# Neighborhood attention on one core: V's lower shift in one DMA, and a band's loads issued earlier

## The chip, the cores and the metric

The kernel runs on one core of a Trainium2 chip. The metric is device time in microseconds (us), from one launch to its end. Engines are named as the profile names them: PE is TensorE's matmul (PEld its weight load), DVE is VectorE, ACT is ScalarE, POOL is GpSimd, and SP is SyncE, which here only issues DMAs.

## The reference

The image is 224 x 224 with 192 channels in bf16. Every pixel attends to 49 neighbours, a 7 x 7 window with dilation 2, shifted inward at the edges. There is one head.

```
qkv = x @ wqkv;  q, k, v = split(qkv)
r0 = clip(row - 6, 0, H - 13);  c0 = clip(col - 6, 0, W - 13)
neighbours of (row, col): rows r0 + 2a, columns c0 + 2b,  a, b in 0..6
p = softmax(q . k[neighbours] * C**-0.5)
out = (p @ v[neighbours]) @ wo
```

## The kernel before

Because of the dilation a pixel sees only pixels of its own row parity (apart from the edges), and the same for columns. The work is therefore cut into a row class `rc` (2), a column class (2) and tiles of 8 x 8 queries of one class. The weights are folded at the start: the logits are x times G, where G is computed from x and wq wk', and the values carry wv wo in them, so that no separate output projection is left.

**Steps and pairs.** There are 14 *steps* (`n` in the code), one for a band of 32 image rows and a row class: `steps[n] = (ti, rc)`. A step has 7 *pairs* (`m` = 0 to 6), and the main loop runs over all 98 pairs with a running number `k`. A pair has two slots (`ab`), each a column of two 8 x 8 query tiles for both column classes. For a pair the kernel does:

- `stage1`: matmuls of x and G into the logits (line 499), and the row maximum on DVE (line 501).
- `stage1b`: the exponential on ACT (line 508), once for each slot.
- `stage2`: the transpose of the probabilities, on PE with a copy by DVE (lines 538 and 539), or, for pairs 4 and 5 of steps 2 to 10 (table `TURN`), by a DMA transpose on SP's queue (line 522).
- `stage3`: the product with V (line 549), three pairs later (`LAG = 3`).
- `stage4`: division by the row sum on DVE (lines 555 and 572) and an output DMA, on SP's queue for most (line 578), from six rotating buffers `o_sb`.

**Background work.** Between the stages of the current pairs the kernel prepares the next step: G's tiles (`g_items`; evacuated by ACT, part of it copied on by POOL, line 450) and V's 14 blocks (`v_item`; matmuls in lines 335 and 338, evacuated by ACT or DVE, lines 326 and 328). Which item runs behind which pair is written out by hand in the strings `BACK` (steps 2 to 11) and `LATE`. The preparation of a step begins in pair 3 of the step before it and ends in pair 2 of the step itself. In `BACK` the items v0 to v6 come up to the first item of pair 6, v7 and v8 later in pair 6, v9 in pair 0, and v10 to v13 in pair 1.

**V's lower shift.** A step's keys are two half-bands of eight rows. V is kept in two tiles for each row class, and each newly made V has its lower 64 partitions copied into the lower partitions of the other tile (`v_over`, line 349). The 14 blocks stand at places 0 to 13 of a tile, and the list `AT` says which block stands where: a slot s reads the places `AT[s - 1]` and `AT[s]`, so that the first slot of a step reads the places 7 (block 13) and 0, and the eighth is the first that reads place 8. The list `vs` makes the blocks in the order 0 to 6, 13, 7 to 12, so that its first eight items, v0 to v7, fill the places 0 to 7. `back` starts the shift in parts, when the last item of a part has been evacuated.

**Loads.** A band of x is read from HBM by three DMA transposes on SP's queue (`load_items`, line 154): tile `x1`, from which POOL copies the `xb` rows (line 160) and sorts columns into `xs` (line 170), and the two `xa` tiles. `x1` has two buffers, so the load of band n + 3 overwrites that of band n + 1, which POOL must have read. The list `ld` holds the three loads of a step, and one is taken off and issued at the end of each of the pairs 0, 1 and 2.

**What sets the order.** Each engine runs its instructions in the order of the program (`in_order`). SP's queue holds, in that order, the outputs, V's shift, the loads and the DMA transposes of the probabilities; each issue also waits until the DMA issued eight places before it has landed. POOL's queue holds the copies of G, V's last shift, the copies and sorts of x, and the output DMAs of the first slot of a step (line 601).

Of the kernel before, what the change touches and what calls it, by code (L numbers as in the profile page):

```python
# [99 lines left out]
def kernel(  # L100
# [44 lines left out]
    def load_items(b):  # L145

        src = xp[16 * b:16 * b + 16].rearrange("r j c -> (r j) c")
        at = (16 * b) % (2 * RP) * S

        def one(k):  # L150
            if k == 1:
                X1[b] = x1_p.tile([128, BND], BF, name=f"x1_{b}", tag="x1")
            dst = X1[b][:] if k == 1 else XA[k // 2][:, at:at + BND]
            nc.sync.dma_start_transpose(out=dst.unsqueeze(1), in_=src[:, 128 * k:128 * k + 128])  # L154

        return [lambda k=k: one(k) for k in ((0, 2, 1) if b in (0, 2, 3) else (1, 0, 2))]
# [183 lines left out]
    def v_item(rc, ti, cb):  # L340
        def emit(dve):
            pv = ps_g.tile([128, 512], F32, name="pv", tag="pg")
            v_mms(pv, lambda k, h: XS[rc][:, k, cb, 64 * h:64 * h + 64])
            evac(_win(VV[rc][ti % 2], 0, 128, AT[cb] * VP, [[193, 2], [1, C]]), pv[:, 0:2 * C].rearrange("p (t c) -> p t c", c=C), dve)
        return emit

    def v_over(rc, ti, c0, c1, eng=nc.sync.dma_start):

        eng(out=VV[rc][1 - ti % 2][0:64, c0:c1, :], in_=VV[rc][ti % 2][0:64, c0:c1, :])
# [126 lines left out]
    def stage1(J, ab):  # L476
        s = 2 * J.m + ab
        s_ps = SS[ab]


        cols = {0: [(1, 7, S - 7), (8, 8, 0)], 2: [(1, 15, 9)]}.get(s, [(2, 14, 8 * s - 6)])
        lo = cols[0][0]
        for cc in range(2):
            units = []
            for h in range(2):
                u = []
                for pas in range(2):
                    X = (XA, XB)[pas][cc]
                    for (v, k0, n) in key_rows(J, h):
                        for (q, nq, c) in cols:  # L490
                            o = _win(s_ps, 64 * h, 64, cc * 256 + 16 * k0 + q, [[16, n], [1, nq]])
                            u.append((n * nq, o, G[J.rc][cc][:, pas, s, 64 * h:64 * h + 64], _win(X, 0, 128, _x(J.rc, v, c), [[RW, n], [1, nq]]), pas))
                units.append(u)
            done = [0, 0]
            while units[0] or units[1]:
                h = 0 if units[0] and (done[0] <= done[1] or not units[1]) else 1
                (cols_, o, w, r, pas) = units[h].pop(0)
                done[h] += cols_
                nc.tensor.matmul(o, lhsT=w, rhs=r, start=(cc == 0 and done[h] == cols_), stop=(cc == 1 and not units[h]), skip_group_check=True)  # L499
        nmx = stat.tile([128, 2], F32, name="nmx", tag="nmx")  # L500
        nc.vector.tensor_reduce(out=nmx[:], in_=_win(s_ps, 0, 128, lo, [[256, 2], [16, 16], [1, 16 - lo]]), axis=AX.XY, op=ALU.max, negate=True)  # L501
        J.p = PP[J.k % 3]
        J.s[ab] = (s_ps, nmx)

    def stage1b(J, ab):
        s_ps, nmx = J.s[ab]
        for cc in range(2):
            nc.scalar.activation(out=J.p[:, ab, cc].rearrange("p q (r k) -> p q r k", k=8), in_=_win(s_ps, 0, 128, cc * 256, [[8, 2], [16, 16], [1, 8]]),  # L508
                                 func=ACTF.Exp, bias=nmx[:, cc:cc + 1], scale=1.0)
# [3 lines left out]
    def turned(J):  # L513
        return J.m in TURN[J.n]
# [97 lines left out]
    def g_all(n):  # L612
        ti, rc = steps[n]
        its = [g_items(rc, ti, s0, ns) for (s0, ns) in GROUPS]
        return [it for (w0, w1, h) in its for it in (w0, w1)], [h for (w0, w1, h) in its]
# [31 lines left out]
    def pool_do(n):  # L647
        for _ in range(min(n, len(pool_q))):
            pool_q.pop(0)()
# [51 lines left out]
    ld, gw, vs = [], [], []  # L701

    def back(it, by_dve):
        it(by_dve)
        for (i, c0, c1) in ((7, 0, 8), (10, 8, 11), (13, 11, 14)) if nb == 0 or nb >= 11 else ((6, 0, 6), (9, 6, 10), (13, 10, 14)):
            if it in vs and it is vs[i]:
                v_over(rcb, tib, c0, c1, pool if nb >= 11 or nb > 0 and i in (13,) else nc.sync.dma_start)

# [6 lines left out]
    for k in range(NP + 2):  # L715
        J = pairs[k] if k < NP else None
        n = J.n if J else NSTEP
        w64, w128 = [], []
        if J:
            m = J.m  # L720
            nb, mb = divmod(k - LAG, 7)
            bg = k >= LAG and nb + 1 < NSTEP
            if bg and mb == 0:
                tib, rcb = steps[nb + 1]
                gw, gh = g_all(nb + 1)
                vs = [v_item(rcb, tib, cb) for cb in (0, 1, 2, 3, 4, 5, 6, 13, 7, 8, 9, 10, 11, 12)]
            if n == 0:
                w64 = gh0[m + 1:m + 2] if m < 3 else gh[mb // 2:mb // 2 + 1] if mb % 2 == 0 else []
                w64 = [(it, False) for it in w64]
            elif bg:  # L730
                w = [(({"g": gw, "h": gh, "v": vs}[t[0]][int(t[1:].rstrip("de"))], t[-1] == "d" or t[-1] == "e" and turned(pairs[k - 1])) if t != "-" else None) for t in (SECOND if nb == 0 else BACK if nb < 11 else LATE)[mb].split()]
                w64, w128 = [it for it in w[:1] if it], w[1:]
            stage1(J, 0)
            stage1(J, 1)
            stage1b(J, 0)
            if m == 0 and n + 3 < NBAND:
                ld = load_items(n + 3)
        if k == NP:
            stage2(pairs[k - 1])
        late = [pairs[i] for i in values_of(k)]  # L740
        for A in late[:1]:
            stage3(A, 0)
            stage3(A, 1)
            if k >= NP:
                stage4a(A, 0)
                stage4a(A, 1)
            stage4(A, 0)
            if k == NP - 1:
                stage4a(A, 1)
        for (it, by_dve) in w64:  # L750
            back(it, by_dve)
        if J:
            stage1b(J, 1)
        if J and turned(J):
            stage2(J)
        if 1 <= k < NP and not turned(pairs[k - 1]):
            stage2(pairs[k - 1])

        if late and n > 0:
            stage4(late[0], 1)  # L760
        for A in late[1:]:
            stage3(A, 0)
            stage3(A, 1)
            stage4(A, 0)
            stage4(A, 1)
        if not J:
            continue

        for w in PLAN[m].split() if n == 0 else ():
            (kind, by), at = w.split(":")[0], [int(c) for c in w.split(":")[1:]]  # L770
            if kind in "VWGH":
                {"V": v0, "W": vs, "G": gw0, "H": gw}[kind][at[0]](by == "d")
            elif kind == "N" and late:
                stage4(late[0], 1)
            elif kind == "X":
                xb_items(2, act if by == "a" else dve)[at[0]]()
            elif kind == "R":
                v_over(0, 0, at[0], at[1], nc.scalar.dma_start if by == "a" else nc.sync.dma_start)
            elif kind == "T":
                v_over(rcb, tib, at[0], at[1], nc.scalar.dma_start if by == "a" else nc.sync.dma_start)  # L780
        for (it, by_dve) in w128:
            back(it, by_dve)
        if ld:
            ld.pop(0)()
        if n == 0 and m == 1:
            first_vd()
            g_row_on(1, 2, 12)
            g_col_on()
        for q in range(2):
            if (n, m) == ((1, 3), (1, 5))[q]:  # L790
                marks_on(q)
        add = [it for c in FIRST[k] for it in first_pool(c)] if k < len(FIRST) else []
        if n > 1:
            if m == 3 and n + 2 < NBAND:
                add = sort_items(n + 2, J.rc, pool)
            if m in (2, 4) and n + 3 < NBAND:
                srt = sort_items(n + 3, J.rc, pool)
                add = srt[:2] if m == 4 else xb_items(n + 3, pool) + srt[2:]
        pool_q[:0] = add
        if n == 12 and m == 1:  # L800
            last = ((0, 9, 0, 1), (9, 7, 9, 0))
            g_col(1, 6, 0, 1, pool)
            g_row(1, 6, 0, 1, pool, last)
            g_row(1, 6, 1, 13, pool, last[1:])
        pool_do(max(4 if n < NSTEP - 1 else 8, len(add)))
# [34 lines left out]
```

## Time and profile before

| | |
|---|---|
| median of 3 runs | 339.31 us |
| the three runs | 339.48, 337.97, 339.31 us |
| the profiled execution | 337.53 us |
| its span, first to last instruction | 335.8 us |
| granted TensorE clock, mean over the span | 0.996 |
| moved by DMA | 55.78 MB, mean 166 GB/s |
| SP's DMA queue, share of 16 engines' span | 84.6% |

The durations below come from the one profiled execution, which was faster than two of the three timed runs. Its span is shorter than its time by what lies before the first instruction and after the last one. In lines of a timeline the columns are start and duration in us, engine and line of the kernel, operation, output and input tile, and in brackets the idle time before it with what ended it. In lines of a list of groups they are line, engine, operation, tiles, shapes and count, then busy us and the mean ns of one, then the idle time before. In a list of waits they are total us, number of times, and the longest.

### The profile page before, as it was taken

How to read it: one execution, taken by the hardware profiler on the slowest of the kernel's cores; microseconds unless marked ns; L12 is line 12 of the kernel's file. 1: busy time of each engine (PE TensorE's matmuls, PEld its weight loads, DVE VectorE, ACT ScalarE, POOL GpSimd, SP SyncE). 2: the span in 40 equal slices, each digit the busy share in tenths (PEclk: the TensorE clock that was granted, in tenths of full speed). 3: DMA queues.
4: the chain of work that ended last, by engine and by line, in shares of the span. 5: the costliest groups of instructions: out<-in, count | busy, mean ns of one | idle time of the engine just before them, and what ended most of it. 6: DMA issues, size and time to landing. Idle time of an engine off the chain costs nothing.

```text
span 335.8 us, 18841 instructions
## 1 busy us (share of the span) xinstructions
PE 318.4 (95%) x7820; PEld 292.8 (87%) x7820; DVE 310.0 (92%) x729; ACT 307.4 (92%) x809; POOL 287.1 (86%) x428
## 2 busy tenths in 40 slices
PE   4699999999999999999999999999999999999982
PEld 3578898999999999998999999989999889999871
DVE  8859999989999999999999999999999999999993
ACT  7679899999999999898999999999999999999992
POOL 8499999899987989789699797997987977997765
PEclk9999999999999999999999999999999999999998
DMA  9999745999999899799997997989989978758934
GB/s 186 215 165 193 141 112 128 208 198 194 182 186 187 160 190 176 140 221 149 169 187 175 179 184 176 163 155 198 174 154 184 182 144 130 143 115 154 149 88 111
DMA packets 143368, 55.78 MB, mean 166 GB/s; under 512 B 117113, under 2 KB 141138, under 8 KB 143283
## 3 DMA queue, kind: packets, MB, share of 16 engines
q1 hardware_dynamic: 138203, 51.98, 84.6%
q0 software_dynamic: 4416, 1.81, 3.0%
q8 instruction: 61, 1.00, 1.2%
q10 hardware_dynamic: 664, 0.80, 1.1%
q14 instruction: 24, 0.20, 0.2%
HBM read 0.29 MB, written 19.27 MB: 58 GB/s over the span
## 4 chain that ended last, share of the span: by engine, by line
PE 80%; ACT 6%; DVE 4%; DMA 3%; SPq 3%; issue 1%; POOL 1%; POOLq 0%; DVEq 0%; ACTq 0%
PE s L499 18%; PE o_ps L549 17%; PE pg L415 13%; PE pv L335 10%; PE pv L338 9%; PE pt_ps L538 7%; PE pgh L415 7%; ACT p L508 3%; SPq L154 3%; DVE nmx L501 2%; DMA pt_sb<-p 2%; DMA xa<-in_x_dram 2%; ACT v L328 1%; ACT g L328 1%; ACT gx L328 1%
## 5 line engine op out<-in xcount | busy, mean ns | idle before, releaser
L508 ACT ACTIVATE p<-s,nmx 128x256 bf16<-128x256 f32 x392 | 163.5, 486 | 15.4 <-DVE nmx L501 13.7
L501 DVE TENSOR_REDUCE nmx<-s 128x2 f32<-128x448 f32 (+1 forms) x196 | 114.3, 624 | 8.9 <-PE s L499 4.5
L572 DVE TENSOR_TENSOR o_sb<-o_ps,rs 128x384 bf16<-128x384 f32 x169 | 94.2, 558 | 5.9
L499 PEld LDWEIGHTS <-g 128*64 128x64 bf16 x2592 | 86.8, 110 | 7.0 <-issue 1.9
L328 ACT CAST v<-pv 128x384 bf16<-128x384 f32 x180 | 85.5, 513 | 2.9 <-PE pv L338 2.4
L499 PE MATMUL s<-xa,g 128*64 128x196 bf16 (+8 forms) x1296 | 83.0, 217 | 1.0 <-ACT p L508 1.0
L499 PE MATMUL s<-xb,g 128*64 128x196 bf16 (+8 forms) x1296 | 82.8, 217 | 0.2 <-ACT g L328 0.2
L549 PE MATMUL o_ps<-v,pt_sb 128*64 128x193 bf16 x1456 | 81.2, 246 | 0.2 <-DMA pt_sb<-p 0.2
L335 PE MATMUL pv<-wb,xs 128*64 128x384 bf16 x406 | 74.6, 333 | 3.7 <-ACT xs L360 3.1
L338 PE MATMUL pv<-wp,xs 128*64 128x192 bf16 x812 | 75.3, 250 | 0.1
L450 POOL COPY g<-gx 64x512 bf16<-64x512 bf16 (+1 forms) x110 | 61.9, 563 | 14.7 <-ACT gx L328 10.6
L601 POOL DMA_DIRECT2D out_dram<-o_s x120 | 68.4, 576 | 3.5 <-issue 2.6
L549 PEld LDWEIGHTS <-pt_sb 128*64 128x64 bf16 x1456 | 66.5, 109 | 0.3 <-DMA pt_sb<-p 0.3
L415 PEld LDWEIGHTS <-aw 128*64 128x64 bf16 x1320 | 58.9, 111 | 8.3 <-issue 2.3
L338 PEld LDWEIGHTS <-xs 128*64 128x64 bf16 x812 | 60.4, 112 | 6.3
L328 ACT CAST g<-pg 128x512 bf16<-128x512 f32 (+4 forms) x130 | 53.8, 480 | 1.4 <-PE pg L415 0.8
L415 PE MATMUL pg<-xb,aw 128*64 128x512 bf16 (+9 forms) x440 | 55.0, 272 | 0.0
L415 PE MATMUL pg<-xa,aw 128*64 128x512 bf16 (+9 forms) x440 | 53.4, 273 | 1.5 <-ACT gx L328 0.9
L170 POOL COPY xs<-xa 128x896 bf16<-128x896 bf16 x51 | 46.6, 941 | 5.5 <-DMA xa<-in_x_dram 4.7
L538 PE MATMUL pt_ps<-ident,p 128*64 128x128 bf16 x1072 | 45.5, 219 | 0.0
L539 DVE COPY pt_sb<-pt_ps 128x1024 bf16<-128x1024 bf16 x63 | 42.9, 681 | 0.3 <-DMA out_dram<-o_sb 0.2
L335 PEld LDWEIGHTS <-xs 128*64 128x64 bf16 x406 | 33.2, 111 | 8.3 <-ACT xs L360 3.5
(78 smaller groups left out, 363.4 us busy)
## 6 DMA issues: line engine op xcount, KB each, us to landing
out_dram<-o_sb SPq DMA_DIRECT2D x156, 96.0 KB
v<-v SPq DMA_DIRECT2D x10, 289.5 KB
v<-v SPq DMA_DIRECT2D x10, 193.0 KB
out_dram<-o_sb SPq DMA_DIRECT2D x13, 78.0 KB
xb<-xb SPq DMA_DIRECT2D x2, 448.0 KB
out_dram<-xs SPq DMA_DIRECT2D x12, 72.0 KB
v<-v SPq DMA_DIRECT2D x2, 337.8 KB
out_dram<-o_s POOLq DMA_DIRECT2D x26, 18.0 KB, 3.3
```

What stands on the lines that cost most here:

```text
L328: nc.scalar.copy(out=out_, in_=in_)
L335: nc.tensor.matmul(pv[64 * h:64 * h + 64, 0:2 * C], lhsT=at(1, h), rhs=WB[:].rearrange("p t c -> p (t c)"), start=True, stop=False, skip_g ...
L338: nc.tensor.matmul(pv[64 * h:64 * h + 64, cc * C:(cc + 1) * C], lhsT=at(2 * cc, h), rhs=WP[(cc, 0)], start=False, stop=True, skip_group_ch ...
L415: nc.tensor.matmul(o, lhsT=l, rhs=r, start=(pas == 0), stop=(pas == 1))
L450: nc.gpsimd.tensor_copy(out=G[rc][cc][p:p + 64, 1, s0:s0 + ns, :], in_=gx[p:p + 64, 0:ns * 128].rearrange("p (s q) -> p s q", q=128))
L499: nc.tensor.matmul(o, lhsT=w, rhs=r, start=(cc == 0 and done[h] == cols_), stop=(cc == 1 and not units[h]), skip_group_check=True)
L501: nc.vector.tensor_reduce(out=nmx[:], in_=_win(s_ps, 0, 128, lo, [[256, 2], [16, 16], [1, 16 - lo]]), axis=AX.XY, op=ALU.max, negate=True)
L508: nc.scalar.activation(out=J.p[:, ab, cc].rearrange("p q (r k) -> p q r k", k=8), in_=_win(s_ps, 0, 128, cc * 256, [[8, 2], [16, 16], [1, ...
L538: nc.tensor.transpose(pt_ps[64 * h:64 * h + 64, 4 * ab + 2 * cc + q, :], J.p[:, ab, cc, q, 64 * h:64 * h + 64], ident[:])
L549: nc.tensor.matmul(o_ps[64 * h:64 * h + 64, cc * 193:cc * 193 + 193], lhsT=J.pt[:, 4 * ab + 2 * cc + q, 64 * h:64 * h + 64], rhs=V[h][:, A ...
L572: nc.vector.tensor_tensor(out=o_sb[:], in0=_win(o_ps, 0, 128, 0, [[194, 2], [1, C]]), in1=rs[:].unsqueeze(2).to_broadcast([128, 2, C]), op ...
L601: pool_q.append(lambda dst=dst, p=p, m=n * nj, cc=cc: nc.gpsimd.dma_start(out=dst, in_=o_sb[p:p + m, cc, :]))
```

## The change

Two parts. For steps 2 to 11 the shift of V was three parts, two DMAs on SP's queue (places 0 to 5, started behind item v6 of `vs`, and places 6 to 9, started behind v9) and a copy on POOL (places 10 to 13, behind v13). It becomes two parts, one DMA (places 0 to 7, behind v7) and a copy on POOL of places 8 to 13, again behind v13. In steps 2 to 10 the three loads of a band are no longer issued at the end of pairs 0, 1 and 2, but behind the first exponential of each of these pairs; on SP's queue each then stands ahead of its pair's two outputs instead of behind them. Steps 0 and 1 and the last steps stay as they were.

```
     def back(it, by_dve):
         it(by_dve)
-        for (i, c0, c1) in ((7, 0, 8), (10, 8, 11), (13, 11, 14)) if nb == 0 or nb >= 11 else ((6, 0, 6), (9, 6, 10), (13, 10, 14)):
+        for (i, c0, c1) in ((7, 0, 8), (10, 8, 11), (13, 11, 14)) if nb == 0 or nb >= 11 else ((7, 0, 8), (13, 8, 14)):
             if it in vs and it is vs[i]:
                 v_over(rcb, tib, c0, c1, pool if nb >= 11 or nb > 0 and i in (13,) else nc.sync.dma_start)
...
             stage1b(J, 0)
             if m == 0 and n + 3 < NBAND:
                 ld = load_items(n + 3)
+            if ld and n > 1:
+                ld.pop(0)()
         if k == NP:
             stage2(pairs[k - 1])
...
         for (it, by_dve) in w128:
             back(it, by_dve)
-        if ld:
+        if ld and n < 2:
             ld.pop(0)()
```

More of the change, by code (lines that the diff above doesn't have):

```diff
@@ L704, in back @@
         it(by_dve)
-        for (i, c0, c1) in ((7, 0, 8), (10, 8, 11), (13, 11, 14)) if nb == 0 or nb >= 11 else ((6, 0, 6), (9, 6, 10), (13, 10, 14)):
+        for (i, c0, c1) in ((7, 0, 8), (10, 8, 11), (13, 11, 14)) if nb == 0 or nb >= 11 else ((7, 0, 8), (13, 8, 14)):
             if it in vs and it is vs[i]:
@@ L737 @@
                 ld = load_items(n + 3)
+            if ld and n > 1:
+                ld.pop(0)()
         if k == NP:
@@ L782 @@
             back(it, by_dve)
-        if ld:
+        if ld and n < 2:
             ld.pop(0)()
```

## The prediction

> **What bounds the kernel now.** I read the page's head first, then a table of busy times by step, because the change touches only steps 2 to 11 and a mean over the span mixes those with the start and the end. A step is one band of 16 rows of one row class (seven pairs of tiles); the bounds of the windows are the starts of the first max-reduction of each step.
>
> ```profile
> span 335.8 us, 18841 instructions
> PE 318.4 (95%) x7820; PEld 292.8 (87%) x7820; DVE 310.0 (92%) x729; ACT 307.4 (92%) x809; POOL 287.1 (86%) x428
> ...
> core 0: us, PE busy (x) PEld busy (x) DVE busy (x) ACT busy (x) POOL busy (x), PEclk, DMA share, GB/s
> 68.94:90.66 21.72, 21.72 (x529) 20.16 (x526) 21.04 (x49) 21.05 (x58) 21.03 (x24) 1.00 1.04 191
> 112.39:134.49 22.10, 22.10 (x585) 20.70 (x582) 21.11 (x50) 20.79 (x57) 20.77 (x28) 1.00 0.98 184
> 134.49:156.97 22.48, 22.39 (x646) 20.97 (x642) 21.11 (x49) 20.72 (x57) 19.05 (x26) 1.00 0.97 166
> 156.97:178.73 21.76, 21.76 (x549) 20.62 (x546) 21.05 (x51) 20.78 (x57) 18.70 (x25) 1.00 0.96 180
> 200.46:222.18 21.72, 21.72 (x529) 20.15 (x526) 21.04 (x50) 20.76 (x57) 19.05 (x26) 1.00 0.92 168
> 222.18:243.90 21.72, 21.72 (x529) 20.14 (x526) 21.04 (x50) 20.76 (x57) 19.05 (x26) 1.00 0.95 177
> ```
>
> The reader is to see three things. PE fills the step: 21.72 of 21.72 us, at a granted clock of 1.00. Steps with the same number of matmuls (529) take the same 21.72 us to the hundredth, while their DMA shares (1.04, 0.92, 0.95) and POOL loads (21.03, 19.05) differ; a step that waited for DMAs or for POOL would not repeat so exactly. And the longer steps are longer by their matmuls: 56 more make 0.38 us (6.8 ns each), 117 more make 0.76 us (6.5 ns each), since the ring of x splits some windows in two there. So in these steps the order of matmuls sets the time, and nothing that shortens SP, POOL or a DMA shows unless PE was waiting for it.
>
> Next, therefore: who waited, between 60 and 270 us.
>
> ```profile
> POOL v L349 <- ACT v L328: 11.2, 8, 2.0
> POOL g L450 <- ACT gx L328: 5.4, 9, 0.9
> POOL xb L160 <- DMA x<-in_x_dram: 3.0, 2, 1.6
> PEld L549 <- DMA pt_sb<-p: 0.3, 1, 0.3
> PE o_ps L549 <- DMA pt_sb<-p: 0.2, 1, 0.2
> ```
>
> Of the waits that this change can reach, only one is PE's: once, for a DMA transpose of the probabilities, 0.3 us. The rest are POOL's, and POOL's idle time is no time of the kernel.
>
> **The change, part by part.** It is made in the built order as the diff says: SP issues ten DMAs fewer, PE, DVE and ACT keep their order to the instruction.
>
> *(a) V's lower shift.* Ten times (for steps 2 to 11) two DMAs of 6 and 4 blocks become one of 8, and POOL's copy grows from 4 blocks (1544 elements) to 6 (2316). No row has 2316 elements:
>
> ```profile
> L349 POOL COPY v<-v 64x1544 bf16<-64x1544 bf16 x10 | 14.7, 1470 | 11.9 <-ACT v L328 11.8
> L349 POOL COPY v<-v 64x3088 bf16<-64x3088 bf16 x2 | 5.5, 2757 | 0.1
> ...
> 163.97 1.47 POOL L349 COPY v<-v 64x1544 bf16<-64x1544 bf16 x1 [1.96 <-ACT v L328]
> 166.01 1.28 POOL L450 COPY g<-gx 64x512 bf16<-64x512 bf16 x2 [0.57 <-ACT gx L328]
> ```
>
> Between the two forms an element costs 1287/1544 = 0.83 ns, so 772 more cost 0.64 us: the copy takes 2.11 us, ten times 6.4 us of POOL. Bounds: nothing (were the copies' length set by the wait before them) and 0.74 us (half of 1.47, with all of it in proportion); I take 0.64, which lies on a line between two measured copies. Where it goes: the copy starts at the same cast of V as now, POOL is then idle 0.57 us before the next copies of G, so these start 0.07 us late, and the slack comes back at the next step's wait of up to 1.96 us. The copied blocks are first read by the second half of the fourth pair, whose products come three pairs later, about 6 x 3.1 us into a step: 175.6 us in step 6, while the copy would end at 163.97 + 2.11 = 166.1. Cost on the path: 0. If that cover is gone, it is 0.64 us a step.
>
> The DMA side. Queued on SP now, in steps 6 and 2, with the products that read the second part (it holds the block that the step's first pair needs) and, last, the cast of V that the new DMA waits for:
>
> ```profile
> 156.85 0.55 SPq L349 DMA_DIRECT2D v<-v  x1
> 157.49 3.69 SPq L578 DMA_DIRECT2D out_dram<-o_sb  x3
> 161.27 0.55 SPq L349 DMA_DIRECT2D v<-v  x1
> 161.91 1.66 SPq L154 DMA_TRANSPOSE x<-in_x_dram  x1
> 166.44 0.26 PEld L549 LDWEIGHTS <-pt_sb 128*64 128x64 bf16 x5
> ...
> 73.96 0.56 SPq L349 DMA_DIRECT2D v<-v  x1
> 78.38 0.28 PEld L549 LDWEIGHTS <-pt_sb 128*64 128x64 bf16 x6
> 156.89 0.53 ACT L328 CAST v<-pv 128x384 bf16<-128x384 f32 x1
> ```
>
> The second part is issued 166.44 - 161.27 = 5.17 us before it is read in step 6, and 4.42 us in step 2. It arrived in time in this execution, since no wait of PE for v stands in the list. After the change everything up to block 7 leaves when its eighth cast ends, 157.42 us in step 6: 9.0 us before it is read. SP saves one issue of 0.55 us a step. The added wait (for the eighth cast instead of the seventh) holds back what is queued behind: the band's load and the outputs. In step 6 the wait ends 0.57 us after the old issue at 156.85, and the outputs that used to follow the DMA now precede it. Cost on the path: 0; gain on the path in this execution: 0.
>
> *(b) The band's loads.* In steps 2 to 10 the three loads leave about a pair earlier: the first one right behind V's DMA, at about 158.0 us instead of 161.91 in step 6. The price is a wait: the load overwrites a buffer that POOL's sort must have read.
>
> ```profile
> 69.09 0.93 POOL L170 COPY xs<-x 128x896 bf16<-128x896 bf16 x1
> 175.73 0.93 POOL L170 COPY xs<-x 128x896 bf16<-128x896 bf16 x1
> ```
>
> In step 7 (from 178.73) that read ends at 176.66, 2 us before the step starts; in step 2 at 70.02, 1.08 us after its start at 68.94, where SP would stand still for up to 0.6 us with two outputs behind it. Those have six buffers, three pairs of 3.1 us, to leave in; cost 0, at worst 0.6 us once. POOL's 3.0 us of waits for the load go, off the path. What is late next on POOL is ACT's cast, as in the other steps.
>
> What PE gains is that SP is no longer behind when the transposes of the probabilities come:
>
> ```profile
> 264.24 5.30 DMA pt_sb<-p
> 269.58 0.31 PEld L549 LDWEIGHTS <-pt_sb 128*64 128x64 bf16 x8 [0.31 <-DMA pt_sb<-p]
> ```
>
> This one landed 5.30 us after its issue, and PE's weights waited 0.31 us. With an issue less and the loads out of the way, it leaves earlier by a good part of a microsecond: -0.3 us. What is late next there is nothing; the matmuls are back to back.
>
> [...] The extra POOL copies run beside VectorE. Its copy of the transposed probabilities, in a window where POOL is busy 8.00 of 8 us and in one where it is busy 4.10:
>
> ```profile
> L539 DVE COPY pt_sb<-pt_ps 128x1024 bf16<-128x1024 bf16 x1 | 0.7, 681 | 0.0
> L539 DVE COPY pt_sb<-pt_ps 128x1024 bf16<-128x1024 bf16 x3 | 2.0, 680 | 0.0
> 152.00:160.00 8.00, 7.91 (x203) 7.16 (x199) 7.65 (x18) 7.29 (x20) 8.00 (x12) 1.00 0.86 144
> 248.00:256.00 8.00, 8.00 (x203) 7.68 (x201) 7.70 (x20) 7.84 (x21) 4.10 (x7) 1.00 0.91 164
> ```
>
> 681 against 680 ns: VectorE does not feel POOL here. [...]
>
> **The sum.** On the profiled execution: (a) 0, (b) -0.3, so 337.53 - 0.3 = 337.2 us (its span of 335.8 plus 1.7 around it). But that execution is not the typical one: the median of the runs is 339.31, 1.8 above. This trace cannot say what the others waited for. It can say what would stall first: V's second part has 4.42 and 5.17 us, and a landing of 5.30 us, as the transpose had, would cost 0.88 + 0.13 = 1.0 us in steps 2 and 6 alone. The change removes these. I take two thirds of that 1.0 as part of the median's excess, and leave the rest of it to causes that the change does not touch: 339.31 - 0.3 - 0.7 = 338.3 us, 0.3% under the median.
>
> **The rivals.**
>
> *It is plainly faster.* The whole 1.8 us are late landings of V and of the transposes, and go: 337.2 us, 0.6% under the median. For it: the short margins above, 0.3 us seen. Against it: steps alike to 0.01 us, and starts and ends of a run that vary too. 0.36.
>
> *POOL's longer copy reaches PE.* POOL is busy 21.03 of 21.72 us in step 2 and 20.77 of 22.10 in step 4; with 0.64 more it is 21.67 and 21.41. It decides where POOL's work exceeds the step, that is from 0.69 us more in step 2, from 1.33 in step 4 and from 2.67 in step 8. If lateness runs through the three loaded steps (2 to 4), it is 3 x 0.64 = 1.9 us, slower: 341.2. For it: 0.05 us are left in step 2. Against it: the other steps have the waits for ACT to take it up, and the earlier loads return 3.0 us to POOL. 0.10.
>
> *VectorE is slowed by the copies.* [...] The 680 and 681 ns speak against it. 0.03. [...]
>
> That the loads or the shift do not move is excluded by the built order.
>
> **How the numbers follow.** Forecast 338.3 with 0.51. The range goes from 336.8 (the faster case, less the spare of 0.4 us by which the fastest run shown, 337.97, lies over the profiled one) to 339.9 (the median plus the 0.6 us of SP's one wait in step 2). It leaves out the slower cases and the edges of the others, under 2 in 10. Half a per cent, 1.7 us, is about what a measurement of this kernel can tell from no change: the three runs lie 1.5 us apart. Faster by over 0.5%: 0.36; within 0.5%: 0.51; slower: 0.13.
>
> **What would show it.** Right: equal steps of 21.72 us again, no wait of PE for pt_sb or v from 60 to 270 us, POOL's copy at 2.1 us with its idle time before G's copies near 0, no wait of POOL for x, the V DMA on SP about 9 us before its first use. Wrong: a PE wait for G (POOL was the bound), a wait of VectorE for an output DMA, or steps of 529 matmuls longer than 21.72 us.

## The result

The changed kernel takes 342.28 us in the median of 6 runs (342.01 to 344.52), the kernel before 339.35 us in 6 runs beside it (337.33 to 339.48). The ratio is 1.0117, with a 95% interval of 1.009 to 1.0144: slower by 1.2%, where the forecast was 338.3 us and at most 339.9. The medians alone lie 2.93 us apart; the ratio is taken over all runs.

The profiled execution of the changed kernel took 343.01 us, 5.48 more than that of before (337.53). So these two executions lie further apart than the medians, and what follows explains their difference. First the head of its page and the busy times by step, with the same columns as in the prediction; the windows shown are steps 2, 3, 4, 6, 8 and 10.

```profile
span 341.2 us, 18828 instructions
PE 318.5 (93%) x7820; PEld 292.9 (86%) x7820; DVE 309.6 (91%) x729; ACT 306.9 (90%) x809; POOL 292.4 (86%) x428
...
69.23:92.40 23.17, 22.20 (x529) 20.52 (x526) 21.08 (x50) 21.03 (x58) 22.48 (x25) 1.00 0.96 177
92.40:114.12 21.72, 21.72 (x529) 20.14 (x526) 20.98 (x51) 20.73 (x57) 19.59 (x26) 1.00 0.91 179
114.12:137.41 23.29, 22.29 (x586) 20.73 (x582) 21.14 (x51) 20.86 (x57) 21.17 (x29) 1.00 0.99 164
159.74:181.48 21.74, 21.74 (x549) 20.60 (x546) 20.97 (x50) 20.72 (x57) 19.02 (x25) 1.00 0.86 167
203.40:225.19 21.79, 21.79 (x529) 20.25 (x526) 20.95 (x51) 20.73 (x57) 19.64 (x26) 1.00 0.96 163
246.92:270.69 23.77, 22.37 (x586) 21.04 (x582) 21.05 (x51) 20.74 (x57) 21.36 (x29) 1.00 0.95 165
```

PE's work is the same (318.5 against 318.4 us), at the same granted clock (0.996 on both pages, 1.00 in each step shown). Step 3 still takes 21.72 us, so the floor has not moved. Three steps carry the loss: step 2 is 1.45 us over that floor, step 4 takes 23.29 instead of 22.10 (1.19 more), step 10 takes 23.77 where its matmuls need 22.10 (1.67 more). Steps 2 to 10 together take 201.46 us against 197.07, which is 4.39 of the 5.48; step 2 starts 0.29 later, and the rest is in the tail. This is a loss by single stalls, not a slower step.

The waits from 60 to 270 us say what stalled:

```profile
POOL v L349 <- ACT v L328: 15.2, 8, 3.2
...
PEld L499 <- issue: 1.5, 1, 1.5
PE s L499 <- issue: 1.4, 1, 1.4
DVE o_sb L572 <- DMA out_dram<-o_sb: 1.3, 1, 1.3
PEld L415 <- issue: 1.2, 1, 1.2
...
POOL xb L160 <- DMA x<-in_x_dram: 0.4, 1, 0.4
```

POOL waits more than before for the cast of V (15.2 us against 11.2), so it is not the bound. PE waits neither for v nor for a DMA transpose. VectorE waits once, 1.3 us, for an output DMA to leave its buffer: one of the three signs that the prediction gave for being wrong. And PE stands still twice, for 1.2 and 1.5 us before a weight load (PEld), with nothing named but "issue", that is, with no releaser in the profile.

**The wait of VectorE, step 2.** The first fence is SP's queue in the changed kernel, then a row of the chain of waits between 84 and 92 us and the stall itself. The second has two rows of the same queue before.

```profile
72.19 0.54 SPq L349 DMA_DIRECT2D v<-v  x1
72.83 4.66 SPq L154 DMA_TRANSPOSE x<-in_x_dram  x1
77.58 1.26 SPq L578 DMA_DIRECT2D out_dram<-o_sb  x2
78.90 1.83 SPq L154 DMA_TRANSPOSE xa<-in_x_dram  x1
80.83 1.62 SPq L578 DMA_DIRECT2D out_dram<-o_sb  x2
82.50 1.73 SPq L154 DMA_TRANSPOSE xa<-in_x_dram  x1
84.32 3.81 SPq L578 DMA_DIRECT2D out_dram<-o_sb  x4
...
84.32 3.90 DMA out_dram<-o_sb
...
88.31 0.56 DVE L572 TENSOR_TENSOR o_sb<-o_ps,rs 128x384 bf16<-128x384 f32 x1 [1.31 <-DMA out_dram<-o_sb]
```

```profile
74.61 2.28 SPq L154 DMA_TRANSPOSE x<-in_x_dram  x1
...
80.06 1.58 SPq L578 DMA_DIRECT2D out_dram<-o_sb  x2
```

The issue of the first load, right behind V's 386 KB, holds SP for 4.66 us; before it was 2.28. Before, too, the load followed a DMA of V within 0.1 us, but that was the second part, of 193 KB. The wait is not POOL's: the read that had to end first was over by about 70.3 us, 2.6 us before the issue began, and in the steps 3 to 10 it was over 3.6 to 6.2 us before. Counted along the queue, the output that leaves at 84.32 is the same one that left at 80.06 before: 4.26 us later, of which 0.29 is the later start of the step. It lands at 88.22, and VectorE, which could have gone on at 87.00, waits for its buffer. PE then follows it with smaller gaps. Over all outputs of a step, the delay against before, taken from the start of the step, is in the mean 3.70 us in step 2, 2.07 in step 3 and 2.95 in step 4.

**PE without a releaser.** The two stalls in PE's weight loads, and the DMA queues in the 7.4 us up to the second one, in the changed kernel and (second fence) at the same place of step 10 before. A queue's columns are packets, MB, and the time of its packets added up, as a share of the time of 16 engines; here it reaches 110.4%.

```profile
128.78 0.42 PEld L415 LDWEIGHTS <-aw 128*64 128x64 bf16 x15 [1.17 <-issue]
257.51 0.54 PEld L499 LDWEIGHTS <-g 128*64 128x64 bf16 x17 [1.54 <-issue]
...
q1 hardware_dynamic: 2885, 1.13, 110.4%
q0 software_dynamic: 140, 0.05, 3.3%
q8 instruction: 1, 0.02, 1.0%
```

```profile
q1 hardware_dynamic: 2436, 1.16, 92.8%
q0 software_dynamic: 161, 0.06, 4.1%
q8 instruction: 2, 0.03, 1.7%
```

The queue q8, whose kind the page gives as "instruction", moves 1.00 MB in 61 packets of 16 KB on both pages, in the steps one about every 5.1 us. PE and PEld have 15,640 of the 18,828 instructions. From these counts comes an estimate: were q8 PE's program, a block would hold 15,640 / 61 = 256 instructions of 16 KB / 256 = 64 bytes, and the 1055 of a step of 21.72 us (529 and 526) would ask for one every 5.3 us. At the second stall the last two blocks came 10.1 us apart (244.85 and 254.94), the later one ended at 256.07, and PE went on 1.44 us later. Counted along PE's rows, its waits included, both stalls stand at the same remainder of a division by 256 (193 and 194), and so do others: 1.08 and 0.50 us in a second profile of the changed kernel, 1.41 with the V part alone, four of 0.31 to 0.81 with the first load alone early, and one of 0.31 before. In all ten, PE went on 1.28 to 1.56 us after a block had ended, and that block's number is the one that the count of instructions, divided by 256, asks for (at the two stalls shown 20 and 45 blocks had ended, and PE's rows stood at 20.76 and 45.75 times 256). From this agreement it is inferred that PE was out of instructions; the profile names no releaser. What kept a block from coming sooner is not in the trace; that q1's packets, the outputs, loads and shifts of SP's queue, took 110.4% of the 16 engines' time in this stretch, against 92.8%, is.

A third stall, of 1.11 us, lies behind the changed steps and is like the 0.31 us seen before:

```profile
322.84 0.86 PE L549 MATMUL o_ps<-v,pt_sb 128*64 128x193 bf16 x16 [1.11 <-DMA pt_sb<-p]
```

### The profile page after: what moved, and what is told of

Read it like the earlier page. It is cut to its first block, busy times and chain, and to the rows that moved or that the text cites. A ratio compares the mean times of both kernels' runs of the same rounds, so it can differ in the third digit from the quotient of the medians.

```text
span 341.2 us, 18828 instructions
## 1 busy us (share of the span) xinstructions
PE 318.5 (93%) x7820; PEld 292.9 (86%) x7820; DVE 309.6 (91%) x729; ACT 306.9 (90%) x809; POOL 292.4 (86%) x428
## 4 chain that ended last, share of the span: by engine, by line
PE 74%; ACT 8%; DMA 4%; DVE 4%; SPq 3%; issue 3%; POOL 2%; POOLq 0%; DVEq 0%; ACTq 0%
PE s L499 17%; PE o_ps L549 16%; PE pg L415 13%; PE pv L335 9%; PE pv L338 8%; PE pt_ps L538 7%; PE pgh L415 6%; ACT p L508 5%; SPq L154 3%; DVE nmx L501 2%; POOL out_dram L601 2%; ACT v L328 2%; DMA xa<-in_x_dram 2%; DMA pt_sb<-p 1%; DMA out_dram<-o_sb 1%
## 5 line engine op out<-in xcount | busy, mean ns | idle before, releaser
L499 PE MATMUL s<-xa,g 128*64 128x112 bf16 (+8 forms) x1296 | 83.5, 217 | 2.2 <-issue 1.4
L499 PE MATMUL s<-xb,g 128*64 128x112 bf16 (+8 forms) x1296 | 83.1, 217 | 0.2 <-ACT g L328 0.2
L338 PE MATMUL pv<-wp,xs 128*64 128x192 bf16 x812 | 74.4, 248 | 0.0
L338 PEld LDWEIGHTS <-xs 128*64 128x64 bf16 x812 | 60.2, 111 | 6.0
L349 POOL COPY v<-v 64x2316 bf16<-64x2316 bf16 (+2 forms) x16 | 31.2, 1950 | 20.7 <-ACT v L328 20.6
```

What stands on the lines that cost most here:

```text
L338: nc.tensor.matmul(pv[64 * h:64 * h + 64, cc * C:(cc + 1) * C], lhsT=at(2 * cc, h), rhs=WP[(cc, 0)], start=False, stop=True, skip_group_ch ...
```

## The experiments

Theory A: the early loads are at fault, and only because they stand close behind V's 386 KB; DMA engines and SP are full at a stretch, and outputs, transposes and PE's program are late. Theory B: the single DMA of V is at fault. Theory C: POOL's longer copy is. Within A: A1, that only the first load counts; A2, that all three do. Each kernel is compared with the kernel before on the same chip. Three chips were used: one (before: 339.98 us) for the V part alone, the loads alone, POOL's longer copy and the early loads with hardly any of V; one (338.19) for the first load alone early, fewer bytes, the changed kernel again and the place of PE's blocks; one (338.28) for the fourth corner, the two later loads early, the same bytes cut in two and the burst twice. The changed kernel's own 1.0117 comes from none of these series, and on the second chip one more execution of it was 0.7% over before. So a difference between ratios of two series shows a direction, and its size only roughly.

**The V part alone.**

```
-... ((6, 0, 6), (9, 6, 10), (13, 10, 14)):
+... ((7, 0, 8), (13, 8, 14)):
```

> The shift of V as changed (one DMA of eight blocks, a POOL copy of six); the loads where they were before. Theory A (the earlier loads are at fault: the first now stands right behind V's DMA, the DMA engines are full for longer at a stretch, and PE's program and the output DMAs arrive late): no change, 338.5 to 339.6 us, no PE idle time over 0.5 us between 60 and 270 us, SP's issue of the first load near 2.1 us as before. Theory B (the single DMA of 386 KB is at fault): 341 to 342.5 us, with idle times of PE as in the changed kernel. Theory C (POOL's longer copy is at fault): also 341 to 342.5, but with waits for POOL.

Measured: 339.28 us, ratio 0.9972 (0.9953 to 0.9991). B falls as a sole cause: with the loads at their old place the single DMA costs nothing, and the kernel is a little faster than before. Of the kernels here that compute everything it has the lowest ratio, 1.4% under that of the changed one. Its profiled execution was the slowest of its 12 (340.69 us) and has one 1.4-us stall of PE for its program and one of 0.7 us for a transpose of the probabilities, so the big DMA leaves little to spare:

```profile
PEld L415 <- issue: 1.4, 1, 1.4
```

**The early loads alone.**

```
         for (i, c0, c1) in ...                    # three parts, as before
+            if ld and n > 1:
+                ld.pop(0)()
...
-        if ld:
+        if ld and n < 2:
```

> The loads as changed; V's shift in its three old parts. The first load now stands between V's first and second DMA, so the second is issued about 1.5 us later. Theory A: slower, 341 to 343 us, with SP's issues of the first load near 3 us and idle times of PE without a semaphore, perhaps also waits for V's second part, which had 4.4 to 5.2 us. Theory B: no change, 338.5 to 339.6 us. Theory C: no change.

Measured: 346.88 us, ratio 1.0212 (1.0179 to 1.0246). Slower still, and by another wait:

```profile
PE o_ps L549 <- DMA v<-v: 5.4, 7, 1.6
```

Here V's second part (places 6 to 9) is issued in pair 0 behind the first load and the outputs, and PE waits for it seven times. So the two parts of the change belong together: with the loads early, V's block 13 (place 7) must leave before them. The changed kernel has no such wait. This run says that the loads' place is costly, but not by which mechanism in the changed kernel.

**POOL's longer copy with DMAs as before.**

```
-... ((6, 0, 6), (9, 6, 10), (13, 10, 14)):
+... ((6, 0, 6), (7, 6, 8), (13, 8, 14)):
```

> Only POOL's copy is lengthened to six blocks: V's shift is a DMA of places 0 to 5, a DMA of places 6 and 7, and the copy; the loads stay where they were. Theory C: 341 to 342.5 us. Theories A and B: 338.5 to 339.6 us, with the copy at 2.11 us and POOL's idle time before it as now.

Measured: 339.83 us, ratio 0.9993 (0.9966 to 1.0021). C falls: POOL's copy of six blocks is free.

**Early loads with hardly any of V in front.**

```
-... ((6, 0, 6), (9, 6, 10), (13, 10, 14)):
+... ((7, 7, 8), (13, 8, 14)):                     # with the early loads
```

The shift of places 0 to 6 is left out, so the kernel no longer computes the reference's values; only its time is of use.

> The changed kernel, but the shift's DMA in steps 2 to 11 moves place 7 alone, an eighth of its bytes: the shift of places 0 to 6 is left out. Theory A, if it takes V's bytes together with the load behind them: 338 to 339.6 us, SP's issue of the first load back to near 2.1 us. If the loads' place alone is enough, as V's bytes do not matter: 341 to 342.5 us. Theory B: 338 to 339.6 us. Theory C: 341 to 342.5 us.

Measured: 338.59 us, ratio 0.996 (0.994 to 0.998). The same early loads cost nothing when one place is in front of them in place of eight. In its list of waits between 60 and 275 us no engine waits for a DMA, and PE has one line:

```profile
PEld L335 <- issue: 0.3, 1, 0.3
```

The outputs leave SP later by 0.85 us in step 2 and 0.36 in step 4 (3.70 and 2.95 in the changed kernel).

**The fourth corner: little of V, loads at their old place.** Again without the shift of places 0 to 6.

```
-... ((6, 0, 6), (9, 6, 10), (13, 10, 14)):
+... ((7, 7, 8), (13, 8, 14)):                     # loads as before
```

> The fourth corner of two by two: V's DMA moves place 7 only (places 0 to 6 of the shift are left out in steps 2 to 11), the loads at their old place. Beside the kernel with the same small shift and early loads (0.996): if the loads' place has no price of its own, the same ratio, 0.994 to 0.998. If early loads bring a gain that V's bytes hide (the forecast's 0.3 us), this one is slower than that one by about 0.1%; if they have a price of their own, faster by 0.2% or more.

Measured: 337.85 us, ratio 0.9985 (0.9962 to 1.0009). With little of V in front, moving the loads early makes 0.9985 into 0.996; with all of it, 0.9972 into 1.0117. The first difference lies across two chips and its intervals touch, so a gain by the early loads as such is not shown; the second, also between series, is six times as large and of the other sign. With V's DMA of this size it takes both, the bytes and the early loads.

**Which of the loads.** First only the first load early, then only the two later ones, each with the merged V.

```
+            if ld and n > 1 and m == 0:
+                ld.pop(0)()
...
-        if ld:
+        if ld and (n < 2 or m > 0):
```

> The changed kernel, but only the first of the three loads is early, right behind V's DMA; the other two are back at the end of pairs 1 and 2. Theory A1 (what harms is the first load right behind the 386 KB of V's DMA): slower as the change, 341 to 342.5 us, with SP's issue of the first load near 3 us. Theory A2 (what harms is that all three loads follow each other closely): between 339 and 340 us.

```
+            if ld and n > 1 and m > 0:
+                ld.pop(0)()
...
-        if ld:
+        if ld and (n < 2 or m == 0):
```

> The merged V shift, the first load at its old place at the end of pair 0, the two later loads early, behind the first exponentials of pairs 1 and 2. Theory A1 (all of the loss is the first load right behind V's DMA): as with the loads at their old place, 0.995 to 0.999, the first load's issue at about 2.5 us. Theory A2 (loads close behind one another and behind V lengthen the full stretch): now the second load follows the first by its pair's outputs no longer, and some of the loss is here too: 1.001 to 1.007.

Measured: 339.42 us, ratio 1.0047 (1.0029 to 1.0065), and 340.69 us, ratio 1.0065 (1.0037 to 1.0093). Against the V part alone (0.9972) that is 0.75% and 0.93%, and all three early are 1.45%. Both lie where A2 put them. A1 falls: the loads of pairs 1 and 2, which leave behind the burst, cost something by themselves, since the kernel with these two early is slower than before on its own chip. How the price divides between the loads is not settled: three chips stand behind these four ratios. How long an issue of the first load holds SP (shortest, median, longest, in ns), before, with it early, with the others early and in the changed kernel, from the rows of line 154:

```profile
L154 SPq DMA_TRANSPOSE x<-in_x_dram x9: 1569/2178/2385, 74.6 to 250.2; - x9
```

```profile
L154 SPq DMA_TRANSPOSE x<-in_x_dram x9: 2660/3267/4086, 71.7 to 247.4; - x9
```

```profile
L154 SPq DMA_TRANSPOSE x<-in_x_dram x9: 1863/2283/3382, 75.4 to 250.6; - x9
```

```profile
L154 SPq DMA_TRANSPOSE x<-in_x_dram x9: 2614/2860/4663, 72.8 to 248.9; - x9
```

So, by the median, the long issue belongs to the load right behind V's 386 KB. Single long ones come elsewhere too: with the V part alone, where the load leaves 2.3 to 2.8 us behind V, the longest is 3821 ns (median 2142), and the two other loads reach 3521 ns before. The long issue is a sign of the full stretch and not the whole of the price, since the kernel with the longest of them in the median (3267 ns) lost no more than the one with a median of 2283 ns.

**The same bytes, cut in two in time.**

```
-... ((6, 0, 6), (9, 6, 10), (13, 10, 14)):
+... ((6, 0, 6), (7, 6, 8), (13, 8, 14)):          # with the early loads
```

> The changed kernel (all three loads early) with V's DMA cut in two: places 0 to 5 leave behind the seventh item as before the change, places 6 and 7 behind the eighth; POOL's copy stays at six places. The bytes and the loads' places are those of the changed kernel, only the time at which three quarters of V's bytes leave is about a pair earlier. Theory A (the burst): the first load finds only 96 KB ahead of it, its issue takes about 2 us instead of 3.1, and most of the loss goes: ratio 0.995 to 1.003. Rival (the sum of the bytes of a step, or the place of the loads as such): as the changed kernel, 1.008 to 1.014.

Measured: 339.45 us, ratio 1.0027 (1.0006 to 1.0048). By the ratios 0.9 of the 1.2% have gone, with the loads where the change puts them and the same bytes in each step. The longest issue of the first load falls from 4663 to 2836 ns. The expectation had one thing wrong: the six places do not leave a pair earlier. SP's queue in step 3, then in step 2:

```profile
93.03 0.56 SPq L349 DMA_DIRECT2D v<-v  x1
93.69 0.55 SPq L578 DMA_DIRECT2D out_dram<-o_sb  x1
94.32 1.17 SPq L349 DMA_DIRECT2D v<-v  x1
95.59 1.98 SPq L154 DMA_TRANSPOSE x<-in_x_dram  x1
...
71.42 2.64 SPq L349 DMA_DIRECT2D v<-v  x2
74.15 2.84 SPq L154 DMA_TRANSPOSE x<-in_x_dram  x1
```

In steps 3 to 10 the parts are 1.3 to 2.2 us apart with one output between them, and these steps lose 0.1 us in all in this profile. In step 2 SP is late and issues both in a row, with the load next, as the change does; there most of what is left of the loss in this profile stands, a wait of VectorE for an output that left at 83.91:

```profile
88.21 0.56 DVE L572 TENSOR_TENSOR o_sb<-o_ps,rs 128x384 bf16<-128x384 f32 x1 [1.76 <-DMA out_dram<-o_sb]
```

**The burst twice, loads at their old place.**

```
                 v_over(rcb, tib, c0, c1, ...)      # merged, loads as before
+                if 0 < nb < 11 and i == 7:
+                    nc.sync.dma_start(out=scr[nb - 1], in_=VV[rcb][tib % 2][0:64, 0:8, :])
```

> The merged V shift with the loads at their old place (which alone was 0.3% faster), and behind it, in steps 2 to 11, a second DMA of the same 386 KB of V into a piece of HBM that nothing reads. Theory A (a stretch in which the 16 DMA engines are full of V's bytes holds up what shares them: the issues of SP, the blocks of PE's program, the outputs): a burst twice as long does by itself what the early loads did, with every load at its old place: ratio 1.005 to 1.02, PE's program arriving late several times (over 2 us of PEld idle with the releaser issue in steps 2 to 10), waits of VectorE for an output or of PE for the transposed probabilities. Rival (the place of the loads is the fault, the bytes only as something that they queue behind): the loads stand where they stood, so no more than the second issue of 0.6 us on SP: ratio 0.996 to 1.002.

Measured: 350.93 us, ratio 1.0377 (1.0344 to 1.041), nearly twice the upper end of what A expected. `scr` is a piece of HBM that nothing reads. Against the V part alone only a second issue and its bytes were added and no load moved; loads, transposes of the probabilities and outputs are late here, and more often than in the changed kernel:

```profile
POOL xb L160 <- DMA x<-in_x_dram: 21.3, 7, 4.1
...
PE o_ps L549 <- DMA pt_sb<-p: 6.4, 8, 1.7
...
DVE o_sb L572 <- DMA out_dram<-o_sb: 3.0, 4, 1.5
```

The issues of the first load are not longer than before (1997 ns in the median), but the outputs leave 4.18 us later in step 2 and 3.1 to 4.5 us later in each of steps 3 to 8. The rival (place alone) falls. One part of the expectation missed: PE's program is hardly late. At the remainder named above PE stalls three times, for 0.26 to 0.51 us, about 1.1 us in all where over 2 were expected. This kernel also moves more bytes in all, 58.75 MB against 55.78, so it shows that late DMAs do this damage, and not that only a bunch of them does.

**Fewer bytes, all earlier.** The DMA takes places 0 to 5 as before, and POOL copies the rest, 6 and 7 behind the eighth item and 8 to 13 behind the last.

```
-... ((6, 0, 6), (9, 6, 10), (13, 10, 14)):
+... ((6, 0, 6), (7, 6, 8), (13, 8, 14)):
...
-  ... or nb > 0 and i in (13,) else nc.sync.dma_start
+  ... or nb > 0 and i in (7, 13) else nc.sync.dma_start
```

> A candidate: the kernel before with less of V's shift on the DMA engines. A DMA of places 0 to 5 behind v6, POOL copies place 6 and 7 behind v7 and 8 to 13 behind v13; the loads as before. If the DMA engines' load is what makes the rare waits: 338 to 339.3 us, faster than before by 0.2 to 0.5%. If POOL becomes the bound (some 0.8 + 0.6 us more a step): over 341 us.

Measured: 337.99 us, ratio 1.0005 (0.9988 to 1.0021). Its profiled execution has all steps at their floor and one stall of PE, 0.3 us. The DMAs move 193 KB a step less than before, and it brings nothing: in the median of before, the DMAs were in time.

**The changed kernel again.** The same kernel, one more execution.

> The changed kernel once more, for a second profile. If the first profile's idle times are the cause of the 1.2%, this one has such again, 3 to 5 us in all in steps 2 to 10: PE without a semaphore wait right after a late block of its program (queue 8), DVE for an output DMA, PE for a transpose of p; if they were chance, it has under 1 us and the same time.

Measured: 340.4 us beside 338.19 of before, 0.7% over it. The stalls are elsewhere than in the first profile: PE for its program 1.08 us at 150.31 and 0.50 at 105.55, 0.7 for a transpose of the probabilities, and step 2 at its floor of 21.7 us. Steps 2 to 10 take 2.7 us more than before; that lies between the 3 to 5 us and the under 1 us that were expected, so the expectation decides nothing. Which arrival is late differs from one execution to the next. Nor is a late one proper to this kernel: the profiled execution of the V part alone, its slowest, lost 2.4 us in the same steps. That the changed kernel has more of them rests on its median.

**The place of PE's blocks.** 64 idle transposes ahead of the main loop, 128 instructions for PE, half a block by the estimate above.

```
+    t = ps_t.tile([128, 8, 128], BF, name="pt_ps", tag="pt")
+    for q in range(64):
+        nc.tensor.transpose(t[64 * (q % 2):64 * (q % 2) + 64, q // 2 % 8, :], ident[:, 64 * (q % 2):64 * (q % 2) + 64], ident[:])
```

> The changed kernel with 64 idle transposes (128 instructions) added on PE at about 11 us, where it waits 3.2 us for the first sort. If PE's idle times without a semaphore are waits for its program, which comes in blocks of 16 KB (256 instructions of 64 bytes), they fall again at the same place of a block, number 193 or 194 of 256 counted from the program's start, that is at other matmuls than before; the time stays at 341.5 to 343 us. If they come from the data, they fall at the same matmuls as before, number 65 or 66 of 256.

The 16 KB in it are q8's packets (61, 1.00 MB); the 256 instructions of 64 bytes are the estimate from 15,640 instructions in 61 packets.

Measured: 341.0 us, ratio 1.0091 (1.0052 to 1.013); step 2 starts 1.6 us later than before, mostly by the added work. Inconclusive: this profiled execution had no stall of PE for its program of over 0.3 us in the steps, so none could be seen to have moved. That the stalls are waits for blocks rests on the remainders and the landings above.

## Why the prediction was wrong

- **The bound** was read rightly. PE's order sets the floor: 21.72 us again in step 3, 318.5 us of PE against 318.4.
- **(a) V's shift** was right in each number that was measured. POOL's copy was put at 2.11 us and is 2110 ns, VectorE's copies beside it stay at 680 ns:

```profile
L539 DVE COPY pt_sb<-pt_ps 128x1024 bf16<-128x1024 bf16 x49 | 33.3, 680 | 1.2 <-PE pt_ps L538 1.1
L349 POOL COPY v<-v 64x2316 bf16<-64x2316 bf16 x9 | 19.0, 2110 | 15.3 <-ACT v L328 15.2
```

  Cost on the path was put at 0; POOL's part alone is 0.9993. The forecast of 0.3% under the median is what the V part alone gives (0.9972). That may be chance: that the gain comes by the late landings that the prediction named was not tried by itself, and the forecast's 0.3 us for the loads is in that sum too.
- **(b) The loads** is the step that failed, in two sentences. "Those have six buffers, three pairs of 3.1 us, to leave in; cost 0, at worst 0.6 us once": the outputs in step 2 left 4.26 us later, and VectorE waited 1.31 us. And "SP is no longer behind when the transposes of the probabilities come ... -0.3 us": SP is further behind. The issues on its queue in steps 2 to 10, added up, take 186.1 us against 175.3, although V has nine issues fewer there; the 27 loads alone take 72.0 us against 57.0. The prediction took the length of an issue as fixed (its one row of a load has 1.66 us) and counted only what was removed; right behind V's DMA of 386 KB the first load's issue took 2.61 to 4.66 us. The -0.3 us should have been about +4.4 us in the profiled execution, and by the ratios +4.9 us (1.45% between the V part alone and the whole change, of 339.35).
- **The overlooked row.** The prediction's first table has DMA shares of 0.92 to 1.04, and it read from equal steps that a step does not wait for DMAs. That was true of the arrivals as they were then ordered, and does not say how much time was left to spare. Bunching eight places into one issue and putting the three loads earlier, behind it, used up that spare; doubling the bunch cost 3.8%. Nor did the prediction count PE's own program (by the inference above, the 1.00 MB of the q8 line of the page) among what comes by DMA.
- **The rivals.** None of the three had this mechanism. That POOL's copy reaches PE gave 341.2 us, near the time measured, and was refuted by its own run; a near number was no evidence for it. That VectorE is slowed by the copies is not seen: its copy of the transposed probabilities takes 680 ns again, and VectorE is busy 309.6 us against 310.0, while POOL's copies take 2110 ns in place of 1470. No run shows a price of POOL's copies on VectorE; the 0.03 that it got was the author's estimate.
- **The signs.** Of the signs of being right, POOL's 2.1 us came, and no wait of PE for v or for the transposes from 60 to 270 us; POOL still waited for x once, 0.4 us. Of the signs against, two came: a wait of VectorE for an output DMA, and steps of 529 matmuls over 21.72 us (23.17, 21.79, and 21.92 in step 7).
- **What is open.** How the loss divides among the kinds of stall, since they fall elsewhere in each execution, and among the three loads; why an issue behind V's DMA lasts longer; and what held a block of PE's program back in the stretch in which q1 took 110.4%.

## What to carry to other kernels

An engine that never waits for a DMA shows that arrivals are in time, not that there is room: where DMA engines are busy nine tenths of a stretch and the issuing queue nearly as much (before: DMA shares of 0.90 to 1.04 in the nine steps 2 to 10, and issues of 175.3 us in their 197.07 us), ask of a moved or merged transfer what stands behind it in that queue and by how much all of it slips. Spread large transfers ahead of others in time (a gap of 1.3 to 2.2 us between six places and two went with a ratio of 1.0027 in place of 1.0117) rather than save an issue. Measure the parts of a change one by one: here, by the ratios, one half gave 0.3% and the other took about 1.4%.

## What the runs showed of the hardware

- The time for which an issue holds its queue is no constant. The same transposing load held SP for 1.57 to 2.39 us before, where 193 KB had been issued right ahead of it, and for 2.61 to 4.66 us where it was 386 KB. With the V part alone, where the 386 KB left 2.3 to 2.8 us ahead, it was 1.65 to 3.82 us.
- Queue q8, "instruction" on the page, moved 61 packets of 16 KB while the kernel ran, in the steps one about every 5.1 us. Ten stalls of TensorE of 0.3 to 1.5 us with the releaser "issue" stood at one place in 256 of its instructions (256 is the estimate 15,640 / 61), each 1.28 to 1.56 us after such a packet had landed. That TensorE waited there for its program is inferred from this.
